# The second group's k: cast on VectorE as it lands, q and k copied one by one, k's transposes behind the first group's last scores

## The chip, the core and the metric

The kernel runs on one core of a Trainium2 chip. The metric is the device time of one execution in microseconds (us); the median of several runs counts. The engines are named as in the profile: PE is TensorE's matmul, PEld its weight load, DVE is VectorE, ACT is ScalarE, POOL is GpSimd, and SP is SyncE, whose queue issues nearly all DMAs.

## The reference

Eight images, twelve heads, 448 tokens, head size 64. Sigmoid attention without a softmax is followed by a token mixer:

```python
scores = q @ k.T / sqrt(64) - log(448)      # per image and head
attn   = 1 / (1 + exp(-scores))
x      = concat_heads(attn @ v)             # 8 x 448 x 768
wq, wk = x @ w_q, x @ w_k                   # 768 -> 64
mixed  = (wq @ wk.T / sqrt(64)) @ x
out    = relu(mixed) @ w_out
```

Inputs and output are float32. The kernel casts to bfloat16 ahead of PE.

## The kernel before

The heads of an image are taken four at a time, so there are 24 groups (0 to 23); "the first group" is group 0, "the second" group 1. A group's 448 tokens are cut into seven blocks of 64.

**A group.** SP loads q, k and v of the group in float32 into a ring of six buffers (`load1`, L155). POOL, or DVE where the load order has a dot, casts them to bfloat16 (`cast1`, L173). PE transposes q and k into PSUM (`transposes`, L197, 28 small products for each of q and k), and a copy takes both at once to the SBUF tile `qk` (`tr`, L234, the copy at L272). Seven score steps follow (`scores`, L280): four products of a block of k with all of q at L284, then one sigmoid of 128x896 on ACT at L289. `values` (L295) multiplies with v at L302. Here, step g.i stands for the score step of group g and block i.

**The first group** has its own path, so that scores start early. Its q is cast in two parts (blocks 0 to 3 and 4 to 6), and its k in two: k0A, blocks 0 to 2, and k0B, blocks 3 to 6. `tr_part` (L755) transposes one part and copies it to `qk` at L758. Steps 0.0 to 0.2 need q and k0A; steps 0.3 to 0.6 need k0B as well.

**What orders the work.** The kernel is scheduled by hand: each engine runs its instructions in the order in which the program emits them. The string `PLAN` (L117) is walked letter by letter. F is a filler product of zeros (L776) that writes the bank pair that comes next, S the next score step, K the transposes and copy of k0B, q and k the transposes of the next group's q or k, and P or p a value step. The beginning is `FFSSFKSFSSqFSkFSFSpFSp`: after step 0.4 come q1's transposes, after step 0.5 k1's, then step 0.6, then step 1.0.

**PSUM** is four bank pairs, handed out in turn (`bank2`, L72; `release`, L84). A score step, a tile of transposes and a value step take one each; a pair goes to the end of the list when the program emits its last reader. Group 1's q and k share one pair, which goes back with the copy at L272.

**Casts and loads.** `ORDER` (L657) lists the loads in the order in which SP issues them. A load is emitted only when the cast of the one six places ahead of it has been (`pump_loads`, L679), and takes a ring buffer in the order in which these were given up. `pump` (L721) emits POOL's casts. A load with a dot, such as `.k2`, is cast on DVE by `cast_one` (L730), after a score step, and only when at least `LAG` = 9 score steps have been emitted since its load was.

In the order of instructions, DVE's beginning is: cast of q0's first part, copies of q0's first part and of k0A, copy of k0B, joint copy of q1 and k1 (L272), cast of k2 (L188). POOL's is: casts of k0A, k0B, q1, k1, v0, q2, v1, k3, q3 and so on.

Of the kernel before, what the change touches and what calls it, by code (L numbers as in the profile page):

```python
# [10 lines left out]
BF16 = mybir.dt.bfloat16  # L11
# [6 lines left out]
def kernel(  # L18
# [12 lines left out]
    nc = tc.nc  # L31
    B, H, S, HD = q.shape
# [3 lines left out]
    P = 128  # L36
    NI, NP = 7, 64
# [10 lines left out]
    def pool(name, bufs, **kw):  # L48
        return ctx.enter_context(tc.tile_pool(name=name, bufs=bufs, **kw))
# [5 lines left out]
    p_qk = pool("qk", 8)  # L55
# [16 lines left out]
    def bank2():  # L72
        n = free2.pop(0)
        return n, pairs[n], pairs16[n]
# [9 lines left out]
    def release(fb):  # L84
        if isinstance(fb, int):
            free2.append(fb)
        elif (fb[0], 1 - fb[1]) in halves:
            halves.remove((fb[0], 1 - fb[1]))
            free2.append(fb[0])
        else:  # L90
            halves.append(fb)
# [18 lines left out]
    def xt(u, j):  # L110
# [4 lines left out]


    PLAN = (  # L117
        "FFSSFKSFSSqFSkFSFSpFSpSqpPpPSPSSkFSpPSFSSabSrPSPSPXSsPSPpPSp"
        "pPpSPSXSwwSSzWWXwWSPPpSPppNSPSqkSXSSpUSPSpMpSPpPSqkSSPSpPMSP"
        "PPPSSWWXSSwWWWSPpcPSdMpSPPPSXSNSxSqkSUSpPSMppSppPSOoSMSOOqSk"  # L120
        "SoOSMrPpSppPSPSPOoSSsSOzXOSCLlLSLSLLSpPPPPcpPSSdOOSOSCNxSOSc"
# [72 lines left out]
    qk = {}  # L194
    ps_qk = {}

    def transposes(ps, t16, r):  # L197

        for x, i in enumerate(range(r.start, r.stop)):
            for g in range(2):  # L200
                for h in range(2):
                    nc.tensor.transpose(
                        ps[HALF[g], h, x * NP : (x + 1) * NP], t16[HALF[h], i, g, :],
                        ident16[HALF[h], HALF[h]],
                    )

    def transposes_whole(ps, t16, r):

        for x, i in enumerate(range(r.start, r.stop)):
            nc.tensor.transpose(  # L210
                ps[:, x * P : (x + 1) * P], t16[:, i].rearrange("p b d -> p (b d)"), ident16,
            )
# [21 lines left out]
    def tr(n, nm, kind):  # L234
        t = "qk".index(nm)
        if kind == "s":
            return
        if kind == "r":
            qk[n] = p_qk.tile([P, 2, 2, NI, NP], BF16, tag="qk", name="qk")
            w = pq[n].rearrange("p e t i d y -> p e (t i d y)").bitcast(F32)  # L240
            for e in range(2):
                nc.vector.transpose(out=qk[n][:, e].rearrange("p t i n -> p (t i n)").bitcast(F32), in_=w[:, e])
            return
        if kind in "cdef":
            assert n in arranged
            w = pq[n].rearrange("p e t i d y -> p e (t i d y)").bitcast(F32)[:, t]
            if t == 0:
                qk[n] = p_qk.tile([P, 2, 2, NI, NP], BF16, tag="qk", name="qk")
            nc.vector.transpose(out=qk[n][:, t].rearrange("p t i n -> p (t i n)").bitcast(F32), in_=w)  # L249
            if kind in "ef":  # L250
                if t == 0:
                    moves.append((n, p_mv.tile([P, 2, 2 * S], BF16, tag="mv", name="mv")))
                nc.vector.transpose(out=moves[-1][1][:, t].bitcast(F32), in_=w)
            return
        t16 = ld.pop((nm + "16", n))
        if t == 0:
            ps_qk[n] = bank2()
        fb, _, ps = ps_qk[n]
        if kind in "abh":
            transposes_whole(ps[:, t], t16, slice(0, NI))  # L260
        else:
            transposes(ps[:, :, t * S : (t + 1) * S], t16, slice(0, NI))
        if t == 1:
            qk[n] = p_qk.tile([P, 2, 2, NI, NP], BF16, tag="qk", name="qk")
            copy = COPY["s" if kind in "jh" else "v"]
            if kind in "abh":
                copy(
                    out=qk[n].rearrange("p h t i n -> p t i h n"),
                    in_=ps[:, :, 0 : 2 * S].rearrange("p t (i h n) -> p t i h n", i=NI, h=2),
                )  # L270
            else:
                copy(  # L272
                    out=qk[n].rearrange("p h t i n -> p t h (i n)"),
                    in_=ps[:, :, 0 : 2 * S].rearrange("p h (t x) -> p t h x", t=2),
                )
            release(fb)
# [357 lines left out]
    def cols(r):  # L634
        return slice(r.start * HD, r.stop * HD)
# [8 lines left out]
        out=ident, in_=ident, compare_op=ALU.not_equal, fill=1.0, base=0,  # L644
# [8 lines left out]
    for t in wqks:  # L653
# [1 line left out]


    ORDER = (  # L657
        "q1 k1 v0 q2 .k2 v1 k3 q3 q4 k4 v2 w0 v3 k5 k6 q5 "
        "v4 q6 v5 k7 v6 q7 w2 q8 q9 w1 k8 w5 v7 w3 w6 w4 "
        "k9 v8 k10 q10 k11 q11 v9 v10 .k12 q12 .k13 q13 v11 q14 k14 v12 "  # L660
        "v13 q15 k15 .q16 v14 .q17 k16 v15 .v16 k17 q18 k18 k19 v17 .k20 q19 "
# [10 lines left out]
    LAG = 9  # L672
    issued = {}
    done = dict.fromkeys("SPqkKxWNUMOCgz", 0)
# [17 lines left out]
    def ready(nm, n):  # L692
        if (nm, n) not in loaded:
            return False
        if nm == "w":
            return True
        back = 4 if nm == "v" else 2
        if n and (nm, n - 1) not in cast:
            return False
        if n >= back and (nm, n - back) not in used:  # L700
            return False
        return nm == "v" or KIND[n] in "qa" or n < 2 or {("q", n - 2), ("k", n - 2)} <= used

    def cast_now(nm, n, e):
        if nm != "w":
            cast1(n, nm, e)
        elif n:
            COPY[e](out=wout16[:, n - 1, :], in_=w32[n - 1])
        else:
            for h in range(2):  # L710
                for g in range(2):
                    COPY[e](
                        out=wqk16[HALF[g], h::2],
                        in_=w32["qk"].rearrange("p (c n) -> p c n", c=NC)[HALF[h], g::2],
                    )
        cast.add((nm, n))
        pump_loads()
# [3 lines left out]
    def pump():  # L721
        while pumped[0] < len(ORDER):
            nm, n = ORDER[pumped[0]]
            if (nm, n) not in OTHERS:
                if not ready(nm, n):
                    break
                cast_now(nm, n, "g")
            pumped[0] += 1

    def cast_one(e):  # L730
        todo = BY[e]
        if not (todo and todo[0] in issued and done["S"] >= issued[todo[0]] + LAG and ready(*todo[0])):
            return False
        nm, n = todo.pop(0)
        assert e == "v" or nm in "vw" or KIND[n] in "qa"
        cast_now(nm, n, e)
        pump()
        return True

    def cast_by_others():  # L740
        while cast_one("s") or cast_one("v"):
            pass
# [3 lines left out]
    for t16, t32, r, e in ((q016, q0, IA, "v"), (q016, q0, IB, "s"), (k016, k0, KA, "g"), (k016, k0, KB, "g")):  # L746
        COPY[e](
            out=t16[:, r].rearrange("p i b d -> p b i d"),
            in_=t32[:, :, cols(r)].rearrange("p b (i d) -> p b i d", d=HD),
# [24 lines left out]
    for t in PLAN:  # L774
# [10 lines left out]
        elif kind == "P":  # L785
            n, i = divmod(c, NI)
# [4 lines left out]
        elif kind in "qk":  # L791
            if t in "rs":
                quads_r.append(c) if t == "r" else None
                if t == "s":
                    quadrants(c, 0)
            tr(c, kind, t)
            if t in "df":
                used.add(("q", c))
# [5 lines left out]
        elif t == "z":  # L804
            n = quads_r.pop(0)
# [62 lines left out]
```

## Time and profile before

| what | value |
|---|---|
| median of 3 runs | 191.03 us (190.49 to 191.83) |
| the profiled execution's own time | 189.1 us |
| its span | 187.0 us |
| PE busy | 174.7 us (93%) |
| ACT busy | 163.5 us (87%) |
| DVE busy | 138.8 us (74%) |
| POOL busy | 107.7 us (58%) |
| q1 and k1: copy at L272 | starts at 11.38, takes 1.09 us |
| granted PE clock, mean | 0.995 |

All times of the profile count from the start of the span, which is the stretch that the profiler records; the rest of the execution's own time lies around it. A row of the timeline gives start, length, engine, line, operation, output and input tiles, how many instructions are merged, and in brackets the idle time before it with what ended that. In a row of busy times by stretch, the number in brackets counts instructions.

### The profile page before, as it was taken

The numbers are of one execution on the slowest core, as the hardware profiler recorded it, in microseconds if no ns is written. First come the engines' busy times: TensorE is split into PE (matmuls) and PEld (weight loads), VectorE is DVE, ScalarE is ACT, GpSimd is POOL, SyncE is SP. The second block draws the span as 40 slices with busy tenths as digits, with TensorE's granted clock in tenths as the row PEclk, the third lists the DMA queues.
The fourth block names the chain that finished last, engine by engine and source line by source line (L and its number), as shares of the span: only waits on it lengthen the run. The fifth ranks groups of instructions, "written<-read, shape, count | busy, mean of one in ns | idle before, by whom it ended". The sixth has DMA issues, their size and how long they took to land.

```text
span 187.0 us, 8500 instructions
## 1 busy us (share of the span) xinstructions
PE 174.7 (93%) x3645; PEld 115.4 (62%) x3648; DVE 138.8 (74%) x211; ACT 163.5 (87%) x210; POOL 107.7 (58%) x145
## 2 busy tenths in 40 slices
PE   7688899989999999999999999999999999999990
PEld 7234556554555554565555776767997989786650
DVE  3234597677878999989898999979868465797810
ACT  4599999999999989999999999998999989975120
POOL 1366698991976999999999884396032910010000
PEclk9999999999999999999999999999999999999998
DMA  5999999975599989999998996984898634603485
GB/s 170 345 341 366 323 368 330 393 271 186 182 307 404 384 284 276 361 337 340 296 278 274 311 407 240 291 282 128 231 348 292 170 96 89 156 23 85 102 238 168
DMA packets 26389, 48.97 MB, mean 262 GB/s; under 512 B 4080, under 2 KB 20208, under 8 KB 26352
## 3 DMA queue, kind: packets, MB, share of 16 engines
q1 hardware_dynamic: 25952, 47.65, 78.6%
q10 hardware_dynamic: 400, 0.79, 1.2%
q8 instruction: 28, 0.46, 1.0%
q14 instruction: 9, 0.07, 0.1%
HBM read 35.78 MB, written 11.01 MB: 250 GB/s over the span
## 4 chain that ended last, share of the span: by engine, by line
PE 69%; DVE 14%; ACT 6%; DMA 4%; issue 3%; SPq 1%; POOL 1%; ACTq 0%; DVEq 0%
PE banks L284 15%; PE banks L302 13%; PE banks L497 13%; PE banks L577 11%; ACT at L289 5%; DMA k<-in_k_dram 4%; DVE qk L218 4%; PE banks L534 3%; DVE xt L311 3%; PE banks L368 3%; PE banks L412 3%; PE banks L342 2%; PE banks L325 2%; DVE mx L440 2%; DVE qk L272 2%
## 5 line engine op out<-in xcount | busy, mean ns | idle before, releaser
L289 ACT ACTIVATE at<-banks 128x896 bf16<-128x896 f32 x168 | 141.5, 927 | 5.3 <-PE banks L284 4.0
L284 PE MATMUL banks<-qk 64*64 64x448 bf16 x672 | 63.1, 359 | 3.5 <-DVE qk L272 0.9
L302 PE MATMUL banks<-at,v 64*64 64x448 bf16 x672 | 46.6, 350 | 0.2
L284 PEld LDWEIGHTS <-qk 64*64 64x64 bf16 x672 | 25.8, 105 | 24.9 <-issue 14.8
L497 PE MATMUL banks<-wout,mx 64*64 64x384 bf16 x672 | 35.5, 323 | 0.1
L188 POOL CAST v<-v 128x896 bf16<-128x896 f32 x22 | 20.4, 931 | 14.1 <-DMA v<-in_v_dram 13.0
L302 PEld LDWEIGHTS <-v 64*64 64x64 bf16 x672 | 23.1, 106 | 7.8 <-issue 1.7
L497 PEld LDWEIGHTS <-mx 64*64 64x64 bf16 x672 | 24.7, 107 | 3.3
L311 DVE CAST xt<-banks 128x896 bf16<-128x896 f32 x20 | 21.6, 1085 | 4.5 <-PE banks L302 4.2
L440 DVE TENSOR_SCALAR mx<-banks 128x1024 bf16<-128x1024 f32 (+2 forms) x21 | 21.1, 1010 | 5.2 <-PE banks L464 3.0
L577 PE MATMUL banks<-wout,mx 128*128 128x384 bf16 (+1 forms) x138 | 24.7, 320 | 0.0
L577 PEld LDWEIGHTS <-mx 128*128 128x128 bf16 x138 | 11.9, 98 | 10.5 <-issue 4.7
L178 POOL CAST qk<-k 128x896 bf16<-128x896 f32 x11 | 13.4, 1218 | 7.8 <-DVE qk L249 5.2
L178 POOL CAST qk<-q 128x896 bf16<-128x896 f32 x13 | 16.0, 1228 | 2.7 <-DVE mx L440 1.5
L249 DVE STREAM_TRANSPOSE qk<-qk 128x448 f32<-128x448 f32 x24 | 14.9, 628 | 0.0
L377 POOL COPY wq<-wqk 64x448 bf16<-64x448 bf16 x6 | 3.3, 554 | 17.4 <-DVE wqk L376 17.1
L153 POOL COPY qk<-swap 32x448 uint32<-32x448 uint32 x20 | 12.1, 606 | 1.2
L506 DVE COPY o<-banks 128x768 f32<-128x768 f32 x9 | 8.6, 952 | 5.1 <-PE banks L497 5.1
L147 POOL COPY swap<-qk 32x448 uint32<-32x448 uint32 x20 | 11.1, 554 | 1.2
L150 POOL COPY qk<-qk 32x448 uint32<-32x448 uint32 x20 | 11.1, 554 | 1.2
L606 ACT COPY o<-banks 128x384 f32<-128x384 f32 x10 | 4.8, 485 | 7.1 <-PE banks L577 4.9
L218 DVE STREAM_TRANSPOSE qk<-qk 32x448 f32<-32x448 f32 x16 | 10.2, 636 | 0.4
(89 smaller groups left out, 227.3 us busy)
## 6 DMA issues: line engine op xcount, KB each, us to landing
q<-in_q_dram SPq DMA_DIRECT2D x24, 448.0 KB, 5.8
v<-in_v_dram SPq DMA_DIRECT2D x24, 448.0 KB, 6.5
k<-in_k_dram SPq DMA_DIRECT2D x23, 448.0 KB, 6.4
out_dram<-o SPq DMA_DIRECT2D x51, 192.0 KB, 4.3
w<-in_moe_w_out_dram SPq DMA_DIRECT2D x6, 384.0 KB, 4.0
wout<-wout SPq DMA_DIRECT2D x12, 96.0 KB, 7.1
out_dram<-o ACTq DMA_DIRECT2D x3, 192.0 KB, 3.2
qk<-mv SPq DMA_DIRECT2D x8, 56.0 KB, 3.9
```

Source lines behind the costliest of these rows:

```text
L153: eng.tensor_copy(out=w[lo, 1], in_=z[lo])
L178: COPY[e](out=f[:, :, "qk".index(nm)].rearrange("p e i d y -> p e y i d"), in_=ld.pop((nm, n)).rearrange("p (y i e d) -> p e y i d", y=2, ...
L188: COPY[e](out=t16.rearrange("p i b d -> p b i d"), in_=ld.pop((nm, n)).rearrange("p b (i d) -> p b i d", i=NI),)
L218: nc.vector.transpose(out=qk[n][other : other + 32, h].rearrange("p t i n -> p (t i n)").bitcast(F32), in_=w[own : own + 32, 1 - h],)
L249: nc.vector.transpose(out=qk[n][:, t].rearrange("p t i n -> p (t i n)").bitcast(F32), in_=w)
L284: nc.tensor.matmul(sc[HALF[h], g, 0:S], qk[n][HALF[g], h, 1, i, :], qk[n][HALF[g], h, 0].rearrange("p i n -> p (i n)"), start=True, stop=True,
L289: nc.scalar.activation(at, sc[:, :, 0:S], ACTF.Sigmoid, bias=attn_bias, scale=attn_scale)
L302: nc.tensor.matmul(ps[HALF[g], h, 0:S], ld["v16", n][HALF[h], i, g, :], ats[n, i][HALF[h], g, :], start=(i == 0), stop=(i == NI - 1),)
L311: COPY[eng](out=xt(u, j)[:, :, 0:S], in_=ps[:, :, 0:S])
L440: nc.vector.tensor_scalar(dst, ps, moe_scale, 0.0, ALU.mult, ALU.max)
L497: nc.tensor.matmul(ps[HALF[x], y, 0:NB], mx[HALF[y], u, b, 64 * (i - 3 * y) : 64 * (i - 3 * y) + 64], wout16[HALF[y], slot(y, b), x * NB : ...
L577: nc.tensor.matmul(ps, mxs[w][:, 2 * S * c + m * P : 2 * S * c + (m + 1) * P], wout16[:, c, w0:w1], start=(c == 0), stop=(c == NC - 1),)
```

## The change

Four edits, all for the second group:

```diff
     PLAN = (
-        "FFSSFKSFSSqFSkFSFSpFSpSqpPpPSPSSkFSpPSFSSabSrPSPSPXSsPSPpPSp"
+        "FFSSFKSFSSqFSFSkFSpFSpSqpPpPSPSSkFSpPSFSSabSrPSPSPXSsPSPpPSp"
...
             transposes(ps[:, :, t * S : (t + 1) * S], t16, slice(0, NI))
+        if n == 1:
+            if t == 0:
+                qk[n] = p_qk.tile([P, 2, 2, NI, NP], BF16, tag="qk", name="qk")
+            nc.vector.tensor_copy(
+                out=qk[n][:, :, t].rearrange("p h i n -> p h (i n)"), in_=ps[:, :, t * S : (t + 1) * S],
+            )
+            if t == 1:
+                release(fb)
+            return
         if t == 1:
...
     ORDER = (
-        "q1 k1 v0 q2 .k2 v1 k3 q3 q4 k4 v2 w0 v3 k5 k6 q5 "
+        "q1 .k1 v0 q2 .k2 v1 k3 q3 q4 k4 v2 w0 v3 k5 k6 q5 "
...
     def cast_one(e):
         todo = BY[e]
-        if not (todo and todo[0] in issued and done["S"] >= issued[todo[0]] + LAG and ready(*todo[0])):
+        if not (todo and todo[0] in issued and done["S"] >= issued[todo[0]] + (LAG if todo[0][1] > 1 else 0) and ready(*todo[0])):
```

- `.k1` hands k1's cast from POOL to DVE. The lag of nine score steps no longer holds for it, so it is emitted after step 0.0. DVE's beginning is then: cast of q0's first part, copies of q0's first part and of k0A, **cast of k1**, copy of k0B, copy of q1, copy of k1, cast of k2. POOL's list lacks k1.
- For group 1, `tr` copies q and k to `qk` with one instruction each, 128x2x448, in place of one joint copy of 128x2x2x448.
- In `PLAN`, k1's transposes stand behind step 0.6 with the filler ahead of it, and no longer between steps 0.5 and 0.6.
- The order of SP's loads is unchanged. Since k1's cast is emitted at another place, the loads of q3, q4 and k4 take other buffers of the ring: q3 that of v0, q4 that of q2, k4 that of k1 (before: k1, v0, q2).

## The prediction

> **What bounds the kernel now.** I read the page's busy shares and groups first, then the busy times by stretch, then the chain that ended last, and at last the order of time from 8 to 14 us. Step g.i is the scores of group g, block i, with its sigmoid; F is a filler product; k0B is the second part (blocks 3 to 6) of the first group's k.
>
> The page's shares of the engines and its costliest group:
>
> ```profile
> PE 174.7 (93%) x3645; PEld 115.4 (62%) x3648; DVE 138.8 (74%) x211; ACT 163.5 (87%) x210; POOL 107.7 (58%) x145
> ...
> L289 ACT ACTIVATE at<-banks 128x896 bf16<-128x896 f32 x168 | 141.5, 927 | 5.3 <-PE banks L284 4.0
> ```
>
> PE (TensorE) and ACT (ScalarE) both work nearly all the time. The 168 sigmoids read 927 ns each, but follow one another faster, since they overlap.
>
> Busy times by stretch (PE, PEld, DVE, ACT, POOL, granted clock, DMA share, GB/s):
>
> ```profile
> 6.80:8.20 1.40, 0.01 (x1) 0.03 (x2) 0.00 (x0) 1.40 (x2) 0.61 (x1) 1.00 1.04 383
> ...
> 20.00:40.00 20.00, 18.92 (x386) 10.79 (x384) 15.87 (x21) 19.88 (x25) 16.99 (x23) 1.00 1.03 359
> 40.00:160.00 120.00, 118.55 (x2556) 80.08 (x2559) 100.79 (x142) 116.14 (x144) 80.31 (x106) 1.00 0.83 268
> 185.00:187.00 2.00, 0.00 (x0) 0.00 (x0) 0.00 (x0) 0.00 (x0) 0.00 (x0) 0.57 0.15 54
> ```
>
> From 20 to 40 us ACT has 0.12 us free of 20; from 40 to 160 PE has 1.45 free of 120 and ACT 3.86. What is lost ahead of 20 us finds little room to be made good. (The first and the last row are for the clock, below.)
>
> The chain that ended last, in order of time (start, length, what):
>
> ```profile
> 2.76 7.11 DMA k<-in_k_dram
> ...
> 9.92 0.94 POOL k L188
> ...
> 10.91 0.45 PE banks L202 x28
> ...
> 11.38 1.10 DVE qk L272
> ...
> 12.53 0.38 PE banks L284 x4
> ...
> 13.79 3.38 ACT at L289 x4
> ```
>
> The landing of k1, its cast on POOL (GpSimd), its transposes, the joint copy of q1 and k1 on DVE (VectorE) and step 1.0 are a chain; but step 1.0 reaches ACT at 12.97 just as ACT is done with step 0.6. The two chains tie.
>
> The order of time around the change:
>
> ```profile
> 8.52 0.38 PE L284 MATMUL banks<-qk 64*64 64x448 bf16 x4
> ...
> 8.70 0.42 DVE L758 COPY qk<-banks 128x512 bf16<-128x512 bf16 x1 [2.54 <-PE banks L210]
> ...
> 8.84 0.39 PE L776 MATMUL banks<-zeros 128*128 128x512 bf16 x1
> 8.96 5.77 ACT L289 ACTIVATE at<-banks 128x896 bf16<-128x896 f32 x7 [0.58 <-PE banks L284]
> ...
> 9.18 0.57 PE L284 MATMUL banks<-qk 64*64 64x448 bf16 x8
> ...
> 9.92 0.93 POOL L188 CAST k<-k 128x896 bf16<-128x896 f32 x1 [0.27 <-DMA k<-in_k_dram]
> ...
> 10.91 0.41 PE L202 MATMUL banks<-ident,k 64*64 64x64 bf16 x28 [0.16 <-POOL k L188]
> 11.11 0.93 POOL L188 CAST v<-v 128x896 bf16<-128x896 f32 x1 [0.25 <-DMA v<-in_v_dram]
> ...
> 13.47 0.63 DVE L188 CAST k<-k 128x896 bf16<-128x896 f32 x1 [0.99 <-DMA k<-in_k_dram]
> ```
>
> ACT has no idle time from 8.96 on. In the timeline of ACT alone its starts are 8.96 (step 0.2), 9.77, 10.57, 11.36, 12.16, 12.97 (step 1.0), 13.79, 14.61: one each 0.80 to 0.82. What feeds it at 9.77 is the DVE copy of k0B at 8.70 and the scores at 9.18 behind it.
>
> **The change part by part.** It moves one cast from POOL to DVE, splits one copy and moves one block of transposes on PE. By the order of instructions of both kernels, nothing else changes on any engine, ACT and SP included.
>
> *1. k1's cast on DVE, ahead of the copy of k0B.* The cast stands in DVE's queue behind the copy of k0's first part (5.80) and in front of the copy of k0B, and waits for k1's DMA. k1 lands at 2.76 + 7.11 = 9.87. The same cast on DVE took 0.63 (row 13.47), so it runs from 9.91 to 10.54. Queued behind it: the copy of k0B, which was ready at 8.70. It starts about 10.48 (two DVE rows may overlap by 0.08: 20.76 + 1.09 = 21.85, the next starts at 21.77; without overlap 10.58). From its start to the next scores passed 9.18 - 8.70 = 0.48, so step 0.3 starts on PE at 10.96 instead of 9.18; from scores to sigmoid passed 12.97 - 12.53 = 0.44, so ACT starts step 0.3 at 11.40 instead of 9.77. **Cost: 1.63** (1.6 to 1.75), all on the path, since ACT ends step 0.2 at 9.88 and then has nothing. Steps 0.0 to 0.2 need only k0's first part and keep their times.
>
> In the rows of before DVE's instructions start in queue order, and none shows a ready one behind one that waits, so this is the step that the trace bears out least. The Trainium skill (Perfetto Trace Analysis, Per-instruction lifecycle) says that DVE, ACT and GpSimd are strictly first in, first out, which speaks against this change; by the rule the sum is the one given here, and if a ready copy could pass the waiting cast it would be nothing.
>
> *2. k1's chain behind step 0.6, and the split copy.* ACT at its pace of 0.80 takes steps 0.3 to 0.6 at 11.40, 12.20, 13.00, 13.80 and wants step 1.0 at 14.60. On PE: q1's transposes come 0.53 after step 0.3 (9.18 to 9.71), at 11.49; q1's copy 0.47 later (10.91 to 11.38), at 11.96. The trace has no DVE copy of 896 elements: between 0.42 (512, L758) and 1.09 (1792, L272), nearest 0.69 (1024, L330); I take 0.62. q1's lies beside steps 0.5 and 0.6 and costs nothing. The F ahead of step 0.6 writes step 0.3's bank pair, free when its sigmoid ends at 11.40 + 0.92 = 12.32; so F 12.36, step 0.6 at 12.68 (0.32 later, as 10.05 to 10.37), k1's transposes at 13.02, k1's copy 13.49 to 14.11, step 1.0 at 14.17, on ACT at 14.61. **Cost: 0.01.** The shorter cast and copy (0.93 to 0.63, 1.09 to 0.62) gain 0.78 and the F and step 0.6 put ahead cost about 0.66; ACT's pace hides both. With no cover left, a copy at 1.09 adds 0.47, one at 0.42 nothing.
>
> *3. Bank pairs.* k1's transposes move behind step 0.6, so q1/k1's pair goes back one step later: step 1.1, and the F ahead of it, now take step 0.6's pair instead. That is free at 13.80 + 0.95 = 14.75; F 14.79, step 1.1 at 15.11, on ACT 0.43 later at 15.54 instead of 13.79. **Cost: 0.12** (0 to 0.2). From step 1.2 on the pairs wait for sigmoids as far back as before.
>
> *4. Loads, POOL and the rest.* SP's order is the same, its waits are not: q3's load waits for v0's cast (12.04) instead of k1's (10.86), q4's for q2's (13.31), and k4's follows q4's at 13.7: up to 1.2 later. The DMA engines are 0.96 to 1.05 busy in these stretches, and q3 lands about 17.3, 6.4 after its issue, behind k3 at 16.2: the queue stays full, cost nothing; without that cover 1.2, inside the 1.75 by which PE wants it later. POOL loses 0.93 at 9.92, but v0 lands only before 11.11, so its casts do not move. k2's cast on DVE slips from 13.47 to 14.1 and ends at 14.7, 1.9 before its transposes are due even at their old 16.59; the weights' load that waits for its buffer goes at 16.07. All nothing.
>
> *5. To the end.* Behind 13.79 the chain holds PE, ACT and DVE only, all moved alike; landings and POOL, which do not move, hold no link there. Payback: none, at most 0.3 of the gaps seen above.
>
> Sum: 1.63 + 0.01 + 0.12 = about +1.75. The profiled execution took 189.1 (span 187.0 and 2.1 around it) and would take 190.85, the span 188.75. It lies 1.93 below the median 191.03 of runs between 190.49 and 191.83; the same addition gives **192.8**.
>
> **The rivals.**
>
> *Step 1.0 is late too.* If k1's copy costs nearer 1.09, or F and step 0.6 take longer, step 1.0 misses ACT's slot: +0.5 or so, 193.3. For: step 2 leaves no slack. Against: the row of 1024 elements at 0.69.
>
> *PE's clock falls.* PE is idle from 6.80 to 8.19, works to 9.23 and would be idle again to 10.96. Against: the clock stayed 1.00 over the first gap, and fell only about 3.4 us behind the last product (last row of the stretches: 0.57). For: only 1.0 of 4.2 us is busy. PE's work from 11.00 to 15.60 is 1.75 + 2.28 = 4.03; at half clock that adds 0 to 4.0, ACT hides some half of it: +2.0, 194.8. The Trainium skill (TensorE: Matmul & The Clock Gate, A second HAM failure mode) tells of a clock that swings where PE idles briefly and often; the gap of 1.40 in this trace did not do so.
>
> *Not slower: k1 has landed when the copy of k0B is due.* Then the cast holds up nothing. It decides at a landing by 8.70 - 0.63 - 0.04 = 8.03; each 0.1 us later costs 0.1. ACT then keeps its pace, step 1.0 comes at about 12.52 by the chain of step 2 and 12.97 stays ACT's limit: +0.0, 191.0. For: the runs before lie 1.3 apart, so landings may differ from the profiled ones. Against: 9.87 is the end of a queue at 1.01 to 1.05 DMA share whose first five loads are untouched; 1.84 us is more than one whole load.
>
> **How the numbers follow.** The sum as worked out: 0.80, its own range 191.9 to 193.6. Step 1.0 late too: 0.07. Clock: 0.07. Not slower: 0.06. One per cent, 1.91 us, is about what a measurement of this kernel can tell from no change; the sum lies 0.16 below that bound, with a scatter of medians near 0.5. So of its 0.80, 0.50 stays within 1% and 0.30 goes over. Slower: 0.30 + 0.05 + 0.07 = 0.42. Faster: 0.02 from the last rival's scatter. Same: 0.50 + 0.02 + 0.04 = 0.56. The range takes in the sum's own, the late step 1.0 and what scatter brings the clock's low end to: 191.7 to 194.1.
>
> **What would show it.** Right: the DVE cast of k1 starts near 9.9, the copy of k0B near 10.5 behind it, ACT idles about 1.5 ahead of step 0.3 near 11.4, step 1.0 runs near 14.6 and 1.1 near 15.5, and every later landmark stands 1.75 later. Wrong: the copy of k0B still near 8.7 (step 1 falls); ACT idle again ahead of step 1.0 or 1.1 by over 0.3 (steps 2, 3); score pairs 0.38 apart instead of 0.19 (clock); a shift at 40 us that has changed by 160 (step 5).

## The result, and the profile after

The changed kernel takes 191.85 us, median of 22 runs (189.45 to 193.37); the kernel before 189.78, also over 22 runs (188.11 to 191.83). The ratio is **1.0099, 95% interval 1.0072 to 1.0127**: 1.88 us of 189.78 (1.37 to 2.41), clear of no change. It leaves out runs over 1.5% above the fastest of their kernel, eight of the changed kernel's 22; the medians of all runs lie 2.07 apart. The median of 191.03 from three runs, to which the prediction added its sum, was 1.25 too high.

The page of the changed kernel, the lines that answer to those of before:

```profile
PE 176.1 (93%) x3648; PEld 116.3 (61%) x3648; DVE 139.9 (74%) x213; ACT 163.7 (86%) x210; POOL 106.9 (56%) x144
...
L298 ACT ACTIVATE at<-banks 128x896 bf16<-128x896 f32 x168 | 141.7, 926 | 7.6 <-PE banks L293 6.6
```

The mean sigmoid is the same, 926 ns. The idle time of ACT ahead of its sigmoids has grown from 5.3 to 7.6 us. The two long stretches:

```profile
20.00:40.00 20.00, 19.04 (x388) 10.99 (x386) 14.56 (x20) 19.88 (x26) 16.18 (x22) 1.00 1.02 357
40.00:160.00 120.00, 117.25 (x2496) 78.16 (x2485) 100.87 (x141) 114.70 (x142) 80.62 (x107) 1.00 0.83 268
```

From 20 to 40 us nothing has changed for ACT: 0.12 free of 20. The loss is ahead of it. The chain that ended last:

```profile
2.76 6.76 DMA k<-in_k_dram
...
9.55 0.04 DVE k L188
9.58 0.51 issue
10.09 0.43 DVE qk L767
...
10.56 0.41 PE banks L293 x4
...
11.00 4.16 ACT at L298 x6
...
15.95 2.54 ACT at L298 x3
```

POOL's cast of k1 and the joint copy have left the chain. In their place stand the landing of k1 (at 9.52), its cast on DVE, which the view names at 9.55 and counts as "issue" to 10.09, the copy of k0B right behind it, and step 0.3. The order of time shows why:

```profile
6.98 0.39 PE L210 MATMUL banks<-ident,k 128*128 128x128 bf16 x4
...
8.41 0.94 POOL L188 CAST q<-q 128x896 bf16<-128x896 f32 x1 [1.55 <-DMA q<-in_q_dram]
...
9.55 0.63 DVE L188 CAST k<-k 128x896 bf16<-128x896 f32 x1 [3.36 <-DMA k<-in_k_dram]
10.09 0.42 DVE L767 COPY qk<-banks 128x512 bf16<-128x512 bf16 x1
...
10.56 0.57 PE L293 MATMUL banks<-qk 64*64 64x448 bf16 x8 [2.54 <-DVE qk L767]
...
11.00 5.05 ACT L298 ACTIVATE at<-banks 128x896 bf16<-128x896 f32 x6 [1.78 <-PE banks L293]
...
11.45 0.62 DVE L266 COPY qk<-banks 128x896 bf16<-128x896 bf16 x1 [0.94 <-PE banks L202]
...
12.97 0.62 DVE L266 COPY qk<-banks 128x896 bf16<-128x896 bf16 x1 [0.90 <-PE banks L202]
...
13.65 0.38 PE L293 MATMUL banks<-qk 64*64 64x448 bf16 x4 [0.45 <-DVE qk L266]
...
14.39 0.38 PE L785 MATMUL banks<-zeros 128*128 128x512 bf16 x1 [0.17 <-ACT at L298]
...
14.70 0.38 PE L293 MATMUL banks<-qk 64*64 64x448 bf16 x4
```

The transposes of k0B started at 6.98, but its copy starts only at 10.09, when the cast is nearly done (they overlap by 0.09). PE has waited 2.54 us and ACT 1.78. The line of ACT merges six sigmoids, 11.00 to 16.05: steps 0.3 to 1.1.

This profiled execution took 191.76 (span 190.0), 2.7 more than the profiled one of before, and more than the medians differ. Its sigmoids are 1.35 later than those of before at step 1.1 and still 1.32 at step 7.0 (47.59 and 48.91); the rest of the growth, to 2.9 at the last sigmoids, comes in pieces of 0.3 to 1.0 later on, each at another place in each execution of these kernels. The largest here is at 121 us, where PE stands for 0.62 us ("issue" in the chain) between two products of one group of four; no row shows what it waited for. Those pieces are left out of what follows.

### The profile page after: what moved, and what is told of

Same layout as the page of the kernel before. It is cut to its first block, busy times and chain, and to the rows that moved or that the text cites. A ratio compares the mean times of both kernels' runs of the same rounds, so it can differ in the third digit from the quotient of the medians.

```text
span 190.0 us, 8505 instructions
## 1 busy us (share of the span) xinstructions
PE 176.1 (93%) x3648; PEld 116.3 (61%) x3648; DVE 139.9 (74%) x213; ACT 163.7 (86%) x210; POOL 106.9 (56%) x144
## 4 chain that ended last, share of the span: by engine, by line
PE 68%; DVE 16%; ACT 5%; issue 4%; DMA 4%; SPq 1%; ACTq 0%; DVEq 0%
PE banks L293 15%; PE banks L506 13%; PE banks L311 13%; PE banks L586 10%; ACT at L298 5%; DMA k<-in_k_dram 4%; DVE xt L320 4%; DVE qk L218 4%; PE banks L543 3%; PE banks L421 2%; PE banks L377 2%; PE banks L351 2%; PE banks L334 2%; DVE mx L449 2%; DVE qk L281 2%
## 5 line engine op out<-in xcount | busy, mean ns | idle before, releaser
L218 DVE STREAM_TRANSPOSE qk<-qk 32x448 f32<-32x448 f32 x16 | 10.2, 636 | 0.4
```

The costliest lines, as they stand in the source:

```text
L218: nc.vector.transpose(out=qk[n][other : other + 32, h].rearrange("p t i n -> p (t i n)").bitcast(F32), in_=w[own : own + 32, 1 - h],)
```

## The experiments

Theory A is the prediction's: the cast waits for k1's landing and holds the copy of k0B. Theory B: the split copies and the later place of k1's transposes cost the time. Theory C: the other waits of the loads do. Theory D came up on the way: PE's clock falls.

**e1, the cast behind the copy of k0B.** All else is the changed kernel, but for one thing in the ring of loads that the expectation below has wrong: since the cast is emitted later, k4's load takes v1's buffer and not k1's (and v2's load k1's).

```diff
-(LAG if todo[0][1] > 1 else 0)
+(LAG if todo[0][1] > 1 else 3)
```

> The changed kernel, but k1's cast stands on DVE behind the copy of k0B instead of ahead of it. Theory A (the cast waits for k1's landing and holds the copy of k0B, so ACT idles ahead of step 0.3): the hole is gone, the copy of k0B starts near 8.7, step 0.3 follows step 0.2 at ACT's pace, and the time is that of the kernel before, +0.1 us (189.9). Theory B (the split copies and k1's transposes behind step 0.6 cost the time): about +1.9, 191.7. Theory C (the loads of q3, q4 and k4, which wait for other casts now, make later work late): the ring is as in the changed kernel, so +1.0 to +1.9.

Measured 0.9992 (0.9966 to 1.0017). The timeline:

```profile
6.44 5.77 ACT L298 ACTIVATE at<-banks 128x896 bf16<-128x896 f32 x7 [0.64 <-PE banks L293]
...
7.50 0.42 DVE L767 COPY qk<-banks 128x512 bf16<-128x512 bf16 x1 [1.55 <-PE banks L210]
...
8.71 0.63 DVE L188 CAST k<-k 128x896 bf16<-128x896 f32 x1 [0.78 <-DMA k<-in_k_dram]
```

The copy of k0B goes at 7.50, the cast, now behind it, waits for its landing until 8.71, and ACT has seven sigmoids on end from 6.44. With the order of two DVE instructions swapped, the whole loss is gone, within the interval. B falls, since e1 has its cause. C falls too: q3's and q4's loads wait for the same casts as in the changed kernel, and k4's goes even later, at 15.81 behind v1's cast (changed kernel: 13.48).

**e2, the cast alone** ahead of the copy of k0B. Against the kernel before:

```diff
-        "q1 k1 v0 q2 .k2
+        "q1 .k1 v0 q2 .k2
...
-issued[todo[0]] + LAG
+issued[todo[0]] + (LAG if todo[0][1] > 1 else 0)
```

> The kernel before with k1's cast on DVE ahead of the copy of k0B, and nothing else: joint copy and old order of PE. Theory A: the copy of k0B starts behind the cast, ACT idles about 1.5 ahead of step 0.3, time +1.6 us (191.4). Theory B: +0.0. Theory C: +1.0 to +1.9, but with step 0.3 not late.

Measured 1.0090 (1.0056 to 1.0124), 1.7 us: A again. The timeline holds one thing more, the fall of PE's clock:

```profile
10.13 0.63 DVE L188 CAST k<-k 128x896 bf16<-128x896 f32 x1 [4.18 <-DMA k<-in_k_dram]
...
11.15 0.76 PE L284 MATMUL banks<-qk 64*64 64x448 bf16 x8 [2.96 <-DVE qk L758]
...
12.76 0.59 PE L284 MATMUL banks<-qk 64*64 64x448 bf16 x4
...
14.83 0.92 ACT L289 ACTIVATE at<-banks 128x896 bf16<-128x896 f32 x1 [0.51 <-PE banks L284]
```

PE waited 2.96 us (the second row, which merges two groups of four products); then a group of scores reads 0.59 instead of 0.38, and step 0.6 comes only at 14.83, 3.25 after step 0.3 at 11.58, where three steps of 0.80 would take 2.40. The busy times by stretch, cut where the granted clock (third column from the right) changes:

```profile
7.98:11.40 3.42, 0.46 (x9) 0.18 (x12) 0.96 (x2) 1.00 (x2) 1.02 (x2) 1.00 1.01 379
11.40:14.81 3.41, 3.41 (x75) 1.65 (x67) 1.04 (x2) 2.64 (x3) 1.78 (x2) 0.50 1.02 356
14.81:18.22 3.41, 3.35 (x74) 1.62 (x75) 0.59 (x2) 3.39 (x5) 3.12 (x3) 1.00 0.98 328
```

PE was busy for 0.46 of 3.42 us, and then ran at 0.5 for 3.41. This is the prediction's second rival, in an experiment.

**e3, split copies and later transposes alone:** the changed kernel with k1's cast on POOL.

```diff
-        "q1 .k1 v0 q2 .k2
+        "q1 k1 v0 q2 .k2
```

> The changed kernel with k1's cast back on POOL: split copies and k1's transposes behind step 0.6 alone; the ring as before. Theory A: +0.1 us (189.9), no hole ahead of step 0.3, step 1.1 about 0.1 late by its bank pair. Theory B: +1.9. Theory C: 0.0.

Measured 0.9977 (0.9952 to 1.0001): B falls a second time. Run once more as e10, the same kernel gave 0.9988 (0.9956 to 1.0020).

> The changed kernel with k1's cast on POOL once more (split copies and k1's transposes behind step 0.6 alone), to tell whether it beats the kernel before. In the second profile of the kernel before, step 1.0 lost 0.4 us to k1's chain, which this order hides: 0.2 to 0.6 us faster, ratio 0.997 to 0.999. If that loss is made up later: 1.000.

Both lean to faster, but neither interval excludes no change. No version here was shown to beat the kernel before.

**e4, the copy of k0B on ACT.** The cast and its wait stay, but nothing that ACT needs stands behind them.

```diff
-            tr_part("k", k016, KB, "v")
+            tr_part("k", k016, KB, "s")
```

> The changed kernel with the copy of k0B on ACT instead of DVE; k1's cast stays where it is on DVE and waits as before, but nothing that ACT needs is queued behind it. Theory A: the hole shrinks to the copy's own 0.5 us on ACT, step 0.3 near 10.0, time +0.2 to +0.4 us (190.1). Theories B and C: +1.5 or more still, since the cast, the copies, the order of PE and the ring are those of the changed kernel.

Measured 1.0037 (1.0005 to 1.0070), 0.7 us; more than the 0.2 to 0.4 expected, but going by the middle values over half of the loss is gone.

```profile
8.63 0.59 ACT L767 COPY qk<-banks 128x512 bf16<-128x512 bf16 x1
9.10 2.57 ACT L298 ACTIVATE at<-banks 128x896 bf16<-128x896 f32 x3
...
9.77 0.63 DVE L188 CAST k<-k 128x896 bf16<-128x896 f32 x1 [3.60 <-DMA k<-in_k_dram]
```

The cast waits until 9.77 as before; ACT does not, apart from the 0.59 of the copy in its own queue.

**A second profile of each kernel,** with no edit.

> The kernel before once more, for a second profile of it. If its profiled execution was a usual one: step 0.2 on ACT at 8.96 and step 0.3 at 9.77 again. If k0B landed late in it: step 0.2 near 8.1 and step 0.3 near 8.9, as in the runs where nothing holds up the copy of k0B.

In the profiled execution of before k0B landed late. In the second:

```profile
6.01 0.61 POOL L747 CAST k<-k 128x512 bf16<-128x512 f32 x1 [0.78 <-DMA k<-in_k_dram]
...
7.32 0.42 DVE L758 COPY qk<-banks 128x512 bf16<-128x512 bf16 x1 [1.29 <-PE banks L210]
...
9.49 0.93 POOL L188 CAST k<-k 128x896 bf16<-128x896 f32 x1 [0.33 <-DMA k<-in_k_dram]
...
10.48 0.41 PE L202 MATMUL banks<-ident,k 64*64 64x64 bf16 x28 [0.21 <-POOL k L188]
...
10.95 1.09 DVE L272 COPY qk<-banks 128x1792 bf16<-128x1792 bf16 x1 [3.21 <-PE banks L202]
...
12.10 0.38 PE L284 MATMUL banks<-qk 64*64 64x448 bf16 x4 [0.25 <-DVE qk L272]
```

k0B's cast starts at 6.01, not 7.52, and its copy at 7.32, not 8.70; in e1, e3 and e10 that copy starts at 7.50, 7.42 and 7.30. In the 14 profiles of this case k0B's cast starts between 6.01 and 7.52; the profile from which the prediction was made has the latest. ACT, alone, takes step 0.2 at 8.13 and step 0.3 at 8.93, without a hole. But then k1's chain (cast 9.49, transposes 10.48, joint copy 10.95, scores 12.10) is the late one:

```profile
12.54 0.92 ACT L289 ACTIVATE at<-banks 128x896 bf16<-128x896 f32 x1
```

That is step 1.0. From 8.93 four steps of 0.80 would have brought it at 12.13; it comes 0.41 later.

> The changed kernel once more, for a second profile. Theory A: the copy of k0B behind k1's cast, ACT idle 1.5 to 2.2 ahead of step 0.3, step 0.3 between 10.9 and 11.6, step 1.1 between 15.0 and 15.8. Theory D: the clock at 1.0, or fallen if PE idles long enough.

```profile
8.76 0.63 DVE L188 CAST k<-k 128x896 bf16<-128x896 f32 x1 [2.34 <-DMA k<-in_k_dram]
9.30 0.42 DVE L767 COPY qk<-banks 128x512 bf16<-128x512 bf16 x1
...
10.21 0.92 ACT L298 ACTIVATE at<-banks 128x896 bf16<-128x896 f32 x1 [0.76 <-PE banks L293]
```

k1 lands earlier, and step 0.3 comes at 10.21, outside the range of 10.9 to 11.6 that was expected. But the distance from the start of the cast to the sigmoid is 1.45, as in the first profile (9.55 to 11.00) and in e2 (10.13 to 11.58). The landing of k1 sets how long ACT waits.

**e5, k1's load one place later,** behind v0's, so that the suspected wait grows.

```diff
-        "q1 .k1 v0 q2 .k2
+        "q1 v0 .k1 q2 .k2
```

> The changed kernel with k1's load put one place later, behind v0's, so that k1 lands one load (about 1.2 us) later; nothing else differs. Theory A (the copy of k0B waits behind the cast, and the cast for the landing): step 0.3 starts about 1.5 after k1's landing, 1.2 later than in the changed kernel, and the time is +1.2 us over it (ratio to before about 1.016). A theory by which the cast on DVE or the order of PE costs the time by itself: no more than the changed kernel, 1.010. Theory D (PE's clock falls when PE idles through a whole counting window): PE idles some 3.7 us here, the clock falls to 0.5 for about 3.4 us in most executions and scores read 0.59 instead of 0.38 each; +0.5 to +1 us more, 1.019 to 1.022.

Measured 1.0235 (1.0181 to 1.0289), 4.5 us, more than the 1.019 to 1.022 expected with D. The cast starts at 10.47, step 0.3 at 12.12. The stretches, cut in the same way:

```profile
7.47:10.88 3.41, 1.03 (x9) 0.43 (x9) 0.41 (x1) 1.67 (x2) 1.97 (x3) 1.00 1.04 363
10.88:14.29 3.41, 2.81 (x42) 1.16 (x42) 1.18 (x3) 2.09 (x3) 0.93 (x1) 0.50 1.01 351
14.29:17.71 3.42, 3.23 (x47) 1.22 (x50) 1.16 (x2) 2.39 (x3) 2.10 (x2) 0.50 1.02 353
17.71:21.12 3.41, 3.41 (x64) 1.81 (x60) 0.00 (x0) 1.74 (x3) 3.27 (x3) 0.50 1.11 303
21.12:24.54 3.42, 2.40 (x57) 1.11 (x50) 2.18 (x2) 3.42 (x5) 2.63 (x6) 1.00 1.02 338
```

Again a stretch in which PE is busy for a small part (1.03 of 3.41), and then the clock at 0.5, this time for 10.2 us.

**e8, e5 with twelve more fillers** on PE between steps 0.2 and 0.3:

```diff
-        "FFSSFKSFSSqFSFSkF
+        "FFSSFKSFFFFFFFFFFFFFSSqFSFSkF
```

> The run with k1's load one place later, with twelve more filler products on PE between steps 0.2 and 0.3, so that PE's clock has no reason to fall. Theory A with D: step 0.3 is as late as in that run, but the clock stays at 1.0, scores read 0.38, and the time is the changed kernel's plus the 1.2 us of the later landing: ratio 1.015 to 1.017 instead of 1.0235. If the 1.0235 came from the later landing itself: 1.022 to 1.025 again.

```profile
8.59 2.98 PE L785 MATMUL banks<-zeros 128*128 128x512 bf16 x13
...
10.86 0.63 DVE L188 CAST k<-k 128x896 bf16<-128x896 f32 x1 [4.84 <-DMA k<-in_k_dram]
...
11.87 0.57 PE L293 MATMUL banks<-qk 64*64 64x448 bf16 x8 [0.30 <-DVE qk L767]
...
12.31 0.92 ACT L298 ACTIVATE at<-banks 128x896 bf16<-128x896 f32 x1 [2.68 <-PE banks L293]
```

PE is busy through the wait, the scores at 11.87 are two groups in 0.57 as at full clock, the mean granted clock is 0.995 instead of 0.970, and cast to sigmoid is 1.45 again (10.86 to 12.31) where e5 took 1.65. Measured 1.0196 (1.0157 to 1.0236): more than 1.015 to 1.017, less than 1.0235, though the intervals overlap. The fall of the clock and the part of the fillers in preventing it are seen in the profiles; its price is not settled by the times.

**e7, the changed kernel with eight more fillers** there:

```diff
-        "FFSSFKSFSSqFSFSkF
+        "FFSSFKSFFFFFFFFFSSqFSFSkF
```

> The changed kernel with eight more filler products of zeros (0.2 us each) on PE between step 0.2 and step 0.3, so that PE works through most of the time in which it would wait for the copy of k0B. Theory A alone: the time of the changed kernel (1.010), since the fillers lie beside the wait. Theory A with D (part of the changed kernel's time is a fallen clock in some of its executions): 0.3 to 0.8 us less, 1.006 to 1.008, and a narrower spread of times. If fillers delay step 0.3 instead: up to +0.5 us more.

Measured 1.0110 (1.0058 to 1.0162). No gain over 1.0099 is seen, though with half a per cent to either side one of 0.3% could not be. **e9**, e2 with nine more fillers at the same place of its `PLAN`, gave 1.0078 (1.0038 to 1.0118) against e2's 1.0090, which tells nothing either way:

> The run with the cast alone, with nine more filler products on PE between steps 0.2 and 0.3. In that run's profile the clock fell to 0.5 for 3.4 us and step 1.0 lost 0.8 us more by it. Theory A with D: the clock stays at 1.0 and the time falls by up to 0.8 us, ratio 1.005 to 1.008. Theory A alone (the fall was that of one execution): 1.009 again.

**The granted clock of the single runs** tells more. In the 12 profiles in which the clock falls only at the end, its mean is 0.992 or more, and so it is in 73 of the 74 runs of before that stand with the experiments. A mean of 0.991 or less was read in 14 of the changed kernel's 22 runs, in 6 of e2's 12, in all 6 of e5 and in one of e4's 12; in none of the 48 of e1, e3, e6 and e10, where nothing holds up the copy of k0B; and in none of the 23 of e7, e8 and e9, which have the fillers. So the clock falls in most executions of the changed kernel, and the fillers keep it up. The 14 runs took 192.16 us in the mean, the other eight 191.31; in e2 it is 191.91 and 190.75. That is not the price of the clock alone, since a later landing of k1 makes the wait longer and the fall likelier at once. How much of the loss is the clock's stays open.

**e6, step 0.2 ahead of k0B's transposes,** on top of e3, against a late k0B:

```diff
-        "FFSSFKSFSSqFSFSkF
+        "FFSSFSKFSSqFSFSkF
```

> Split copies and k1's transposes behind step 0.6 with k1's cast on POOL, as in the run with split copies alone, and step 0.2 ahead of k0B's transposes on PE, so that ACT takes it at its own pace even when k0B lands late. Theory A and a late landing of k0B in some executions: ACT never waits between steps 0.1 and 0.2; 0.0 to 0.5 us faster than that run, ratio to before 0.995 to 0.998. If ACT's start is not what counts there: 0.998 again.

Measured 1.0009 (0.9965 to 1.0052): no gain seen. ACT's start is not what counts there, as far as the interval tells.

## Why the prediction was right or wrong

**Step 1, the cast ahead of the copy: right, by e1, e2 and e4.** From the start of the cast to step 0.3 it gave 1.49 (9.91 to 11.40); the changed kernel in both profiles, e2, e7, e8 and e9 read 1.45. That DVE does not let a ready copy pass a waiting cast was the step that the trace before bore out least; now the copy of k0B starts at 10.09, though its transposes started on PE at 6.98. Here the Trainium skill (Perfetto Trace Analysis, Per-instruction lifecycle: strictly first in, first out) and the trace agree. The size of 1.63 fits the profile of before alone, in which k0B was late: between the second profile of before and the first of the changed kernel, step 0.3 moves from 8.93 to 11.00, by 2.07.

**Step 2, k1's chain: half right.** The copy of 896 elements took the 0.62 taken for it, and step 1.0 follows at ACT's pace (11.00, then 14.21 by ACT's own rows). But the cost of 0.01 left out a gain. In the second profile of the kernel before, k1's chain holds up step 1.0 by 0.41; the tie was that of one execution. Behind the late step 0.3 this no longer shows, so it takes 0.41 off the 2.07.

**Step 3, bank pairs: right.** In e1 the lead over the profile of before drops from 0.93 at step 1.0 to 0.78 at step 1.1; in e3 from 0.75 to 0.60; expected 0.12. In the changed kernel the filler at 14.39 waits for ACT.

**Steps 1 to 3 together** gave +1.75 at step 1.1. Between the second profile of before (13.36: the pair of sigmoids at 12.54 takes 1.74, the last 0.92 of it step 1.1) and the changed kernel (15.14) it is 1.78: the errors of steps 1 and 2 cancel. That is luck, and so is the pair: the four differences between the two profiles of each kernel are 1.78, 1.35, 0.99 and 0.56. The time of 191.85 lies inside the stated range by 0.15 only, since the base of 191.03 was too high.

**Step 4, loads: right.** q3's load goes at 11.76 instead of 10.88. In e1 the loads of q3, q4 and k4 go at 10.90, 12.18 and 15.81, against 9.64, 10.84 and 12.11 in e3, which has the old ring, and neither e1 nor e3 loses anything.

**Step 5, to the end: not refuted.** The ratio gives 1.88 (1.37 to 2.41), near the sum of 1.75. But the 1.88 holds what the fall of the clock adds in most runs, and the sum does not, so some payback is not excluded.

**How the numbers follow: here it failed.** "The sum lies 0.16 below that bound, with a scatter of medians near 0.5. So of its 0.80, 0.50 stays within 1%": with 0.56 for "same", the forecast called a loss too small to be told. Every case but one of 0.06 was slower, by 1.75 or more, and the interval of 22 runs is 0.28% to either side, not 1%. A loss of 0.9% stands three such widths from no change. The step that failed is the one from the sum to the forecast: no run stands behind its one per cent, and the median of many runs is known far more closely than single runs scatter. The sum itself said slower, and slower it was.

**The rivals.** "Step 1.0 late too" did not come about. "PE's clock falls" did: not in the two profiles of the changed kernel, but in 14 of its 22 runs, so 0.07 was far too low. Its ground was a gap of 1.40 over which the clock stayed up; here PE waits 2.54. Its price of +2.0 was too high, as the 14 runs took 0.85 more than the others, and not all of that is the clock. Of "not slower", k1 never landed by 8.03; at its earliest in the changed kernel, 8.76 for the cast, ACT still waited 0.76.

## What to carry to other kernels

An engine's queue is a line. Before an instruction that waits for a DMA goes ahead of another, compare the landing with the time at which the other is ready, and find out who waits for that one; with the two swapped nothing was lost here (e1). Landing times of one profiled execution are a sample: two profiles of one kernel differed by 1.4 us at the place that set the price. The granted clock is worth reading for every run: the two profiled ones of the changed kernel missed what 14 of 22 had. And a difference in time should be held against the interval that the runs will have, not against the scatter of single runs.

## What the runs showed of the hardware

The changes of PE's clock lie on a fixed grid. In e5 the clock was down from 10.88 to 21.12; that is 10.24 us, or three stretches of 3.413. Counted in such stretches, the fall at the end of e5's profile (191.79) is 53 behind its first fall; in e2, the end (188.89) is 52 behind the fall at 11.40, and the return at 14.81 one. In the changed kernel the grid, counted back from the fall at 189.98, cuts the wait (8.03 to 10.56) at 9.07:

```profile
5.66:9.07 3.41, 2.35 (x22) 0.80 (x19) 0.36 (x1) 2.73 (x4) 1.28 (x2) 1.00 1.03 369
9.07:12.49 3.42, 1.93 (x48) 0.99 (x51) 1.59 (x3) 1.64 (x3) 1.61 (x3) 1.00 1.05 389
```

In all 14 profiles the stretches of the grid that end in a fall hold up to 1.31 us of PE's work (0.46 in e2, 1.03 in e5, 1.31 at 184.13 to 187.54 in e7), and those at full clock that do not end in one hold 1.60 or more (1.60 at 183.15 to 186.56 in the changed kernel, 1.62 at 147.65 to 151.06 in e9). So the clock falls not only after full idleness; the border lies between 1.31 and 1.60 of 3.41 us, as far as these profiles show. The grid lies at another place in each execution (boundaries at 7.98 in e2, 7.47 in e5, 9.07 here). Cut at 7.20 and 10.61, a stretch of the changed kernel's profile holds 0.87, and by the border the clock would then have fallen. An estimate from this profile's rows, with every place of the grid equally likely: a fall in 0.5 to 0.7 of executions; 14 of 22 were read.

The Trainium skill (TensorE: Matmul & The Clock Gate, Part 1) speaks of an idle window of about 3.4 us; the grid here agrees in length, but 1.03 of 3.41 us of work did not keep the clock up. Once down, it came back behind a stretch in which PE was listed as busy throughout (3.41, in e2 and e5), and not behind 2.81 and 3.23 of 3.4 in e5.
